# Strided sparse attention into an ELU feed-forward layer: batch 2 transposed by TensorE, some ELU clamps on ScalarE, batch 1 paced later

## The chip, the cores and the metric

The kernel runs on one core of one Trainium2 chip. The metric is the device time of the whole program in microseconds (us). A run also leaves a trace, whose span is about 1.7 us shorter than the time. A run counts as slow when it takes over 1.5% longer than the fastest of its kernel. A ratio is the mean time of one kernel's fast runs over the mean of the other's fast runs in the same rounds, so it is not quite the ratio of the medians that are quoted. The granted clock is the share of its full clock that TensorE was given in a stretch of a trace; where it is well below 1.00 the text calls it low or cold. SBUF is the core's working memory, PSUM the memory into which TensorE writes.

## The reference

Attention over 8 batches, 8 heads, 576 positions, head size 64, then a feed-forward layer on the 4608 tokens. Heads 0 to 3 see the last 32 positions ("local"), heads 4 to 7 every 32nd position ("strided").

```python
scores = np.matmul(q, k.transpose(0, 1, 3, 2)) / np.sqrt(64)
rel = pos[:, None] - pos[None, :]
mask_local = (rel >= 0) & (rel < 32)
mask_strided = (rel >= 0) & (pos[None, :] % 32 == pos[:, None] % 32)
attn = softmax(np.where(mask, scores, -1e9))       # heads 0-3 local, 4-7 strided
x = (attn @ v) as [4608 tokens, 512]
h = x @ w_in                                       # 512 -> 2048
g = np.where(h > 0, h, np.exp(np.minimum(h, 0)) - 1)
out = g @ w_out                                    # 2048 -> 512
```

## The kernel before

Queries and keys must stand with the head dimension on the partitions. For batches below `NPE` this is done by TensorE (a *T piece*: transposes into PSUM, then one VectorE copy each of q and k to SBUF). For the later batches DMA does it, from SBUF to SBUF. Attention of one batch is four head pairs; a pair is two *S pieces* (score matmuls, Exp, mask), each followed later by its *O part* (row sums, values, normalisation). A batch with T pieces runs T0 S0 T1 S0 S1 T2 S1 S2 T3 S2 S3 S3.

```python
def piece_T(P):
    for nm, dst in (("q", P.qT[:, 0:S]), ("k", P.kT[:, PRE:PRE + S])):
        ps = p_a.tile([128, S], BF16, tag="a", name="tp")
        # ... 8 (strided) or 16 (local) nc.tensor.transpose into ps ...
        nc.vector.tensor_copy(dst, ps)

def elu(hps, g):
    e = p_wk.tile([128, CHUNK], F32, tag="he", name="he")
    nc.scalar.activation(e, hps, ACT.Exp)
    e1 = p_wk.tile([128, CHUNK], BF16, tag="he1", name="he1")
    nc.vector.tensor_scalar(e1, e, scalar1=1.0, scalar2=1.0,
                            op0=ALU.min, op1=ALU.subtract)
    nc.vector.tensor_tensor(g, e1, hps, op=ALU.max)
```

The feed-forward layer of the first 512 tokens comes in one chunk: 16 groups of hidden-layer matmuls with ELU (`l1`), then 16 *slots*, each a quarter of an output tile (`l2`). Batch 1's twelve pieces are spread over the slots.

```python
for m in range(MC):
    l1(0, CHUNK, [m], g0[:, m, :], ...)
LATE = 5
for kk in range(CHUNK // 128):
    for part in range(4):
        l2(kk * 128, ..., part, spare=kk == 1)
        i = 4 * kk + part
        upto = first[1] + max(0, n * (i + 1 - LATE) // (16 - LATE))
        if done >= upto:
            flush()                       # the O parts still open
        while done < upto:
            run_piece(pieces[done], lag=1)
            done += 1
        if i == 2:
            fill_pad(2)                   # three small loads
            batch_in[2] = load_batch(2)
```

Everything after that is a stream of *steps*, from step 16 on. A step is one output quarter (`l2`; there are none in steps 16 to 23), then the attention pieces that are due, then one hidden-layer group (`l1`, 8 matmuls of 256 columns) with its ELU. Batch 2's attention has to be done in steps 23 to 29, batch 3's begins at step 32.

```python
dmaT_at[begin[1] + 1] = 2                 # DMA transposes of batch 2, step 17
for st in range(S0, NST):
    if todo:
        l2(*todo.pop(0))
    # ... lo, hi = step range of the next batch; upto as above ...
    while done < upto:
        run_piece(pieces[done], ...)
    l1(t0, TT, ..., p_a if st < S0 + SPT and j % 3 == 2 else None)
    # ... loads and DMA transposes of later batches ...
```

The softmax here doesn't subtract the row's maximum and nothing guards it: scores larger than these inputs give would overflow.

## Time and profile before

The median is 347.69 us of 3 runs (346.36 to 348.78); the traced run has a span of 346.4 us.

| stretch of the trace | what runs | what TensorE loses |
|---|---|---|
| 0 to 26 us | loads, attention of batch 0 | waits for loads; the change does not touch it |
| 26 to 42 us | hidden layer of the first chunk | little; VectorE is nearly full |
| 42 to 66 us | 16 slots with batch 1's attention | 1 us for ELU, then small gaps |
| 66 to 95 us | end of batch 1, steps 16 to 26, start of batch 2 | waits and a cold clock |
| 105 to 290 us | steady state | about 1% |
| 290 us to the end | the last output tiles | 4.8 us, much the same after the change |

The busy time by stretch of the kernel before. Columns: the stretch and its length, then the busy time and number of instructions of TensorE's matmuls (PE), weight loads, VectorE (DVE), ScalarE (ACT) and GpSimd; the granted TensorE clock; the DMA share; GB/s.

```profile
core 0: us, PE busy (x) PEld busy (x) DVE busy (x) ACT busy (x) POOL busy (x), PEclk, DMA share, GB/s
42.00:50.00 8.00, 6.95 (x45) 3.08 (x43) 5.30 (x11) 1.39 (x3) 2.95 (x4) 1.00 1.85 158
50.00:66.00 16.00, 14.49 (x220) 7.87 (x223) 9.39 (x19) 9.71 (x20) 11.40 (x16) 1.00 1.43 156
66.00:70.00 4.00, 1.67 (x26) 1.22 (x26) 2.55 (x6) 3.18 (x8) 3.65 (x5) 1.00 1.15 178
70.00:78.20 8.20, 7.68 (x53) 5.88 (x52) 5.61 (x11) 3.58 (x6) 2.75 (x4) 0.79 1.73 141
78.20:88.00 9.80, 5.05 (x47) 2.94 (x48) 4.15 (x9) 2.90 (x5) 1.38 (x2) 0.65 1.84 125
```

From 66 to 70 us TensorE is busy 1.67 of 4 us, and in the next stretch the clock is at 0.79; from 78.2 to 88 us it is busy 5.05 of 9.8 us, and the clock is at 0.65 in that stretch itself. A busy TensorE at clock 0.79 also does less: the 7.68 us of the fourth row hold only 53 recorded matmuls.

TensorE's waits, longest in total first, without the first loads at the start: instruction and line, what it waited for, us in total, times, longest.

```profile
...
PE sc L327 <- DMA ksT_114<-ks_89: 3.8, 1, 3.8
PE s_ps L370 <- DVE pm L343: 2.0, 4, 0.9
...
PE sc L327 <- ACT e L335: 1.4, 2, 0.7
PE sc L327 <- DMA klT_116<-kl_91: 1.4, 1, 1.4
...
PE ops L469 <- DVE g_511 L432: 1.0, 2, 0.8
```

TensorE in order of time near the longest wait: start, duration, line, names, count, and in brackets the idle time just before.

```profile
69.95 6.74 PE L441 MATMUL hps<-xT,w_in_sb 128*128 128x256 bf16 x45 [0.91 <-DVE xT L393]
77.20 1.03 PE L441 MATMUL hps<-xT,w_in_sb 128*128 128x256 bf16 x8 [0.52 <-DVE g L432]
82.03 0.42 PE L327 MATMUL sc<-qsT_113,ksT_114 64*128 64x72 bf16 x8 [3.79 <-DMA ksT_114<-ks_89]
...
83.55 1.89 PE L441 MATMUL hps<-xT,w_in_sb 128*128 128x256 bf16 x8
```

Batch 2's first score matmuls (`sc`) wait 3.79 us for a DMA transpose. Directly after it, 8 hidden-layer matmuls take 1.89 us; the same 8 took 1.03 us before the wait.

The chain of waits passes through another of batch 2's transposes, that of its local keys (`klT`), and the DMA view counts the packets:

```profile
62.44 8.72 DMA ks_93<-in_k_dram
72.43 6.02 DMA kl_95<-in_k_dram
78.44 15.59 DMA klT_116<-kl_91
```

Batch 2's queries and keys had landed by 65.4 us at the latest (the last is issued at 58.15 us and takes at most 7.2), before its transposes are issued from 67.15 us on. So TensorE waits for the transposes, which share the DMA engines with batch 3's loads, and not for batch 2's short loads.

```profile
DMA packets 104867, 36.16 MB, mean 104 GB/s; under 512 B 87296, under 2 KB 100224, under 8 KB 104832
```

### The profile page before, as it was taken

What the parts mean: (1) busy time and instruction counts of PE and PEld (TensorE: products, weight loads), DVE (VectorE), ACT (ScalarE), POOL (GpSimd) and SP (SyncE); (2) the same over time, 40 slices, a digit from 0 to 9 for tenths busy, and PEclk for the clock granted to TensorE, in tenths of its full rate; (3) what the DMA queues carried; (4) which work ended last, traced back from release to release, by engine and by line L of the source; (5) the groups of instructions that cost most, each with busy time, mean ns of one, the idle gap of its engine ahead of it and who ended that gap; (6) DMA issues with size and microseconds to landing.
All of it is one profiled execution on the core that took longest, in us unless ns stands there. A gap on an engine that the chain in (4) does not pass through costs nothing.

```text
span 346.4 us, 7372 instructions
## 1 busy us (share of the span) xinstructions
PE 315.0 (91%) x2835; PEld 196.6 (57%) x2880; DVE 233.7 (67%) x465; ACT 198.9 (57%) x377; POOL 80.0 (23%) x106
## 2 busy tenths in 40 slices
PE   1779989784899999999999999999999999999994
PEld 0554444462556666666566666666666666666661
DVE  2577955764687787676867778677767776666650
ACT  1575625742686676565655767676757675444431
POOL 7723246831073081102503034100000000000000
PEclk9999999986999999999999999999999999999999
DMA  6999999999999699911969329911921101111111
GB/s 87 153 206 207 175 169 160 149 148 134 109 144 172 113 106 134 195 42 35 132 116 150 79 45 174 158 38 32 153 55 38 38 22 42 46 32 30 40 53 62
DMA packets 104867, 36.16 MB, mean 104 GB/s; under 512 B 87296, under 2 KB 100224, under 8 KB 104832
## 3 DMA queue, kind: packets, MB, share of 16 engines
q0 software_dynamic: 68256, 18.58, 56.0%
q1 hardware_dynamic: 36576, 17.11, 28.6%
q8 instruction: 22, 0.36, 0.5%
q14 instruction: 13, 0.11, 0.1%
HBM read 37.09 MB, written 9.44 MB: 134 GB/s over the span
## 4 chain that ended last, share of the span: by engine, by line
PE 76%; DMA 11%; DVE 7%; issue 2%; POOL 2%; ACT 1%; DVEq 0%; POOLq 0%
PE hps L441 33%; PE ops L469 33%; DMA klT_116<-kl_91 5%; PE sc L327 3%; DVE g_511 L432 3%; DMA ks_93<-in_k_dram 3%; DMA kl_91<-in_k_dram 2%; PE s_ps L354 2%; DMA kl_95<-in_k_dram 2%; PE s_ps L370 2%; PE o_ps L375 1%; PE o_ps L363 1%; PE tp L292 1%; DVE kT_103 L299 0%; ACT osb L474 0%
## 5 line engine op out<-in xcount | busy, mean ns | idle before, releaser
L441 PE MATMUL hps<-xT,w_in_sb 128*128 128x256 bf16 (+1 forms) x1086 | 151.5, 285 | 2.0 <-DVE xT L393 0.9
L469 PE MATMUL ops<-w_out_sb,g 128*128 128x512 bf16 x473 | 124.8, 381 | 2.1 <-issue 0.2
L428 ACT ACTIVATE he<-hps 128x512 f32<-128x512 f32 x144 | 86.0, 597 | 63.9 <-PE hps L441 59.2
L441 PEld LDWEIGHTS <-w_in_sb 128*128 128x128 bf16 x1088 | 101.3, 99 | 36.2 <-issue 5.7
L469 PEld LDWEIGHTS <-g 128*128 128x128 bf16 x512 | 50.3, 98 | 35.1 <-issue 0.6
L335 ACT ACTIVATE e<-sc 72x576 bf16<-72x576 f32 (+1 forms) x60 | 38.6, 643 | 30.2 <-PE sc L327 30.1
L381 ACT ACTIVATE ln<-s_ps 128x288 f32<-128x288 f32 x64 | 26.2, 410 | 23.9 <-PE s_ps L354 14.0
L474 ACT COPY osb<-ops 128x512 f32<-128x512 f32 x36 | 21.1, 585 | 19.2 <-PE ops L469 18.9
L383 ACT ACTIVATE rc<-ln 128x288 f32<-128x288 f32 x64 | 28.3, 443 | 2.0
L87 POOL DMA_DIRECT2D vs<-in_v_dram x8 | 5.7, 707 | 69.8 <-PE o_ps L363 52.9
L388 DVE TENSOR_TENSOR xT<-o_ps,rc 128x288 bf16<-128x288 f32 x32 | 14.6, 458 | 9.3 <-ACT rc L383 8.5
L337 DVE TENSOR_TENSOR pm<-e,mask_s 72x576 bf16<-72x576 bf16 x32 | 14.6, 455 | 8.6 <-ACT e L335 7.7
L393 DVE TENSOR_TENSOR xT<-o_ps,rc 128x288 bf16<-128x288 f32 x32 | 14.6, 456 | 7.3 <-ACT rc L383 7.1
L128 POOL DMA_DIRECT2D vl<-in_v_dram x8 | 9.4, 1181 | 35.8 <-PE o_ps L375 31.9
L343 DVE TENSOR_TENSOR pm<-e,mask_l 128x576 bf16<-128x576 bf16 x32 | 14.7, 459 | 3.8 <-ACT e L335 3.2
L469 PE MATMUL ops<-w_out_sb,g_511 128*128 128x512 bf16 x60 | 15.3, 380 | 1.9 <-DVE g_511 L432 1.0
L370 PE MATMUL s_ps<-pm,ones 128*64 128x288 bf16 x64 | 10.5, 325 | 2.2 <-DVE pm L343 2.0
L375 PE MATMUL o_ps<-pm,vl 128*64 128x96 bf16 x192 | 11.1, 217 | 0.6 <-ACT ln L381 0.3
L370 PEld LDWEIGHTS <-ones 128*64 128x64 bf16 x64 | 3.8, 109 | 13.3 <-issue 10.5
L354 PEld LDWEIGHTS <-ones 72*64 72x64 bf16 x64 | 3.6, 110 | 13.1 <-issue 12.3
L354 PE MATMUL s_ps<-pm,ones 72*64 72x288 bf16 x64 | 10.7, 332 | 0.3 <-DVE pm L337 0.3
L375 PEld LDWEIGHTS <-vl 128*64 128x64 bf16 x192 | 9.3, 116 | 2.4 <-DVE vl L135 1.1
(379 smaller groups left out, 325.5 us busy)
## 6 DMA issues: line engine op xcount, KB each, us to landing
out_dram<-osb SPq DMA_DIRECT2D x32, 144.0 KB
vs<-in_v_dram POOLq DMA_DIRECT2D x8, 288.0 KB, 7.1
vl<-in_v_dram POOLq DMA_DIRECT2D x8, 288.0 KB, 7.8
w_in_sb<-in_moe_w_in_dram POOLq DMA_DIRECT2D x4, 512.0 KB, 13.7
w_out_sb<-in_moe_w_out_dram POOLq DMA_DIRECT2D x4, 512.0 KB, 20.2
qs_88<-in_q_dram POOLq DMA_DIRECT2D x4, 288.0 KB, 8.6
ks_89<-in_k_dram POOLq DMA_DIRECT2D x4, 288.0 KB, 9.7
qs_92<-in_q_dram POOLq DMA_DIRECT2D x4, 288.0 KB, 8.5
```

The costliest lines, as they stand in the source:

```text
L335: nc.scalar.activation(e[0:R], sc[0:R, :, 0:W], ACT.Exp, scale=scale)
L337: nc.vector.tensor_mul(pm[0:R].rearrange("p z (i n) -> p (z i) n", n=RS), e[0:R].rearrange("p z (i n) -> p (z i) n", n=RS), mask_s.unsquee ...
L343: nc.vector.tensor_mul(pm, e, mb.unsqueeze(1).to_broadcast([128, 2, W]))
L354: nc.tensor.matmul(s_ps[x * D:(x + 1) * D, :].rearrange("p (z n) -> p z n", z=2), lhsT=ones[0:RS, :], rhs=pv[:, x], start=True, stop=True, ...
L370: nc.tensor.matmul(s_ps[x * D:(x + 1) * D, :], lhsT=ones, rhs=pm[:, x], start=True, stop=True, skip_group_check=True)
L375: nc.tensor.matmul(o_ps[x * D:(x + 1) * D, i * LQ:(i + 1) * LQ], lhsT=batch_in[P.b]["vl"][:, (P.g0 + x) * LB + 3 * u + i, :], rhs=pm[:, x, ...
L381: nc.scalar.activation(ln, s_ps, ACT.Ln)
L383: nc.scalar.activation(rc, ln, ACT.Exp, scale=-1.0)
L428: nc.scalar.activation(e, hps, ACT.Exp)
L441: nc.tensor.matmul(hps[:, i], lhsT=w_in_sb[:, cc, m * 128:(m + 1) * 128], rhs=xT[:, cc, t0:t0 + nt], start=(c == 0), stop=(c == KC - 1))
L469: nc.tensor.matmul(ops, lhsT=g[:, m, :], rhs=w_out_sb[:, m, :], start=(m == 0), stop=(m == MC - 1))
L474: nc.scalar.copy(o_sb, ops)
```

## The change

The intent: take batch 2's transposes away from the DMA queue, relieve VectorE while ELU of the first tokens fills it, and leave two slots after batch 1's last piece to cover its latency. With e = exp(h), Relu(1 - e) on ScalarE is 1 - min(e, 1), the negative of what VectorE's clamp gives, so VectorE is left with one instruction per tile. Cut to its core:

```diff
-NPE = 2
+NPE = 3                        # batch 2: long loads, T pieces; its pad loads go
-    def elu(hps, g):
+    def elu(hps, g, on_act=False):
         nc.scalar.activation(e, hps, ACT.Exp)
+        if on_act:
+            nc.scalar.activation(e1, e, ACT.Relu, bias=1.0, scale=-1.0)
+            nc.vector.scalar_tensor_tensor(g, e1, -1.0, hps, op0=ALU.mult, op1=ALU.max)
+            return
-        l1(0, CHUNK, [m], g0[:, m, :], ...)
-    LATE = 5
+        l1(0, CHUNK, [m], g0[:, m, :], ..., on_act=m % 2 == 1)
+    LATE, END = 8, 14
-            upto = first[1] + max(0, n * (i + 1 - LATE) // (16 - LATE))
+            upto = first[1] + max(0, min(n, n * (i + 1 - LATE) // (END - LATE)))
             if i == 2:
-                fill_pad(2)
                 batch_in[2] = load_batch(2)
-    dmaT_at[begin[1] + 1] = 2
-            lo, hi = begin[b - 1] + (7 if b == 2 else 0), begin[b] - 2
+            lo, hi = begin[b - 1] + (4 if b == 2 else 0), begin[b] - 2
         l1(t0, TT, ...,
+           on_act=st < S0 + SPT and j % 2 == 1)       # every other step of 16 to 23
-            if load_at[st] == 3:
-                fill_pad(3)
+            if NPE <= load_at[st] < NPE + 2:
+                fill_pad(load_at[st])
```

Batch 2 now has twelve pieces instead of eight and begins at step 20.

More of the change, by code (lines that the diff above doesn't have):

```diff
@@ L432, in elu, with l1 @@
         nc.vector.tensor_tensor(g, e1, hps, op=ALU.max)
-    def l1(t0, nt, ms, g, pool=None):
+    def l1(t0, nt, ms, g, pool=None, on_act=False):
         hps = (pool or p_h).tile([128, len(ms), nt], F32,
@@ L444, in l1 @@
                     start=(c == 0), stop=(c == KC - 1))
-        elu(hps.rearrange("p a b -> p (a b)"), g)
+        elu(hps.rearrange("p a b -> p (a b)"), g, on_act)
     out_v = out.rearrange("(b p s) f -> b s p f", b=B, s=NS)
@@ L492 @@
     for m in range(MC):
-        l1(0, CHUNK, [m], g0[:, m, :], p_a if m % 5 > 1 else None)
-    LATE = 5
+        l1(0, CHUNK, [m], g0[:, m, :], p_a if m % 5 > 1 else None, on_act=m % 2 == 1)
+    LATE, END = 8, 14
     for kk in range(CHUNK // 128):
@@ L544 @@
            g[:, nm * j:nm * (j + 1), :].rearrange("p a b -> p (a b)"),
-           p_a if st < S0 + SPT and j % 3 == 2 else None)
+           p_a if st < S0 + SPT and j % 3 == 2 else None,
+           on_act=st < S0 + SPT and j % 2 == 1)
         if st in load_at:
-            if load_at[st] == 3:
-                fill_pad(3)
+            if NPE <= load_at[st] < NPE + 2:
+                fill_pad(load_at[st])
             batch_in[load_at[st]] = load_batch(load_at[st])
```

## The prediction

> **What bounds the kernel now.** TensorE is busy 315.0 of 346.4 us (busy totals). From 105.5 to 290 us it is busy 182.8 of 184.5 us (busy time by stretch), and neither the change's code nor its operands reach that part. What can be won lies before 105.5 us:
>
> - 42.1 to 105.5 us. Its warm work, from single durations in the timeline: 23 quarter output tiles at 0.865, 15 hidden-layer groups at 0.87, batch 1 attention about 8.0 us (3.1 of it transposes), batch 2 attention 4.9 us. Sum 45.9 of 63.4 us, so 17.5 us are lost.
> - 78.2 to 94.3 us: TensorE waits 3.79 us for a DMA transpose of batch 2's strided keys, 0.73 for an Exp, and 1.41 for that of the local keys; it is busy only 5.05 of 9.80 us to 88.0, at a granted clock of 0.65. The chain of waits names the same: 8.7 us load of keys, 6.0 us load of local keys, 15.6 us transpose.
> - 66 to 70 us: 0.69, 0.19, 0.87 and 0.91 us of waits on the latency chain of batch 1's last pieces; the clock then falls to 0.79, and 45 matmuls take 6.74 us where 4.9 would do.
> - 42 to 47 us: 1.0 us waiting for VectorE, which is 97% busy from 30 to 40 us with ELU (0.43 clamp + 0.69 max per tile against 0.865 us of matmuls).
>
> **What the change does.** It removes batch 2's four DMA transposes, issued from 67.1 to about 82.3 us, delays its three pad loads, and replaces eight loads of 256-byte runs by two of 1 to 2 KB runs: 87,296 of 104,867 packets are now under 512 B, a size that the Trainium skill, "DMA: Bandwidth & Descriptors", Specifications, puts below line rate. The pads occupy the queue from 36.2 to 43.4 us, so I expect batch 2 landed by about 62 us, before its first use near 70.
> It adds 96 TensorE transposes, 3.1 us (as batch 1's), and eight VectorE copies, 5.6 us (0.45 each, 1.43 for local keys), and packs batch 1's twelve pieces into six slots: about 3 us of small stalls, estimated from copy and Exp latencies.
> Relu on ScalarE: I estimate 0.6 to 0.7 us, as Exp has 0.60. It relieves VectorE by 0.43 on every other early tile and makes ScalarE nearly full; worth 1 to 1.3 us near 45 us.
>
> **Where it lands.** Hidden layer after batch 1 resumes near 68.4 instead of 69.95 us, at full clock (1.9 us more). Steps 20 to 23 are VectorE-bound, about 2 us per step. The first pieces of batch 2 no longer wait for DMA: about 8 us with the recovered clock, minus 3.1 us of transposes and 1.5 of new stalls. What ended at 105.5 us should end at 95 to 98.6. The remaining 241 us is unchanged.
>
> The clock part follows the Trainium skill, "TensorE: Matmul & The Clock Gate", Part 1: idle windows throttle the array. This trace agrees: 0.65 granted exactly where it waited.
>
> **Prediction:** 338.5 us, range 333.5 to 343.5 (8 in 10). Faster by over 2% (under 340.7): 0.68; within 2%: 0.31; slower: 0.01.
>
> **Signs.** Right: no wait of batch 2's score matmuls for a transpose; granted clock near 1.00 from 70 to 90 us; DMA transposes of batch 3 done before step 32; output matmuls no longer wait for the first ELU. Wrong: TensorE waiting for VectorE copies or score buffers between 50 and 66 us; batch 2's loads landing after 70 us; a clock drop still present there.
>
> **What would break it.** Stalls of the packed pieces could eat the gain in 50 to 66 us; VectorE could stay the limit in steps 16 to 24; batch 3's or batch 4's loads, delayed by the pads that moved, could put a new wait near 100 to 160 us.

## The result, and the profile after

The changed kernel takes 343.98 us (median of 4 runs, 343.36 to 344.51) against 347.85 us (4 runs) of the kernel before; ratio 0.9892, 95% interval 0.9853 to 0.9931. It is faster by about 1%, which is "within 2%", and the time lies just above the stated range. Run again in a later group on another chip it took 344.01 us, but the kernel before took 345.32 us there (11 runs), ratio 0.9959. The changed kernel repeats well; the kernel before moves by 2.5 us between groups. So the gain is 1.3 to 3.9 us, where 9.2 us were forecast.

The busy time by stretch after the change, columns as before:

```profile
42.00:50.00 8.00, 8.00 (x46) 3.74 (x45) 2.10 (x4) 2.55 (x5) 3.83 (x5) 1.00 1.70 183
50.00:66.00 16.00, 12.48 (x234) 7.71 (x233) 11.51 (x24) 10.13 (x21) 7.24 (x10) 1.00 1.40 184
66.00:70.00 4.00, 3.54 (x38) 2.59 (x36) 1.53 (x4) 2.86 (x7) 3.86 (x6) 1.00 1.93 132
70.00:78.20 8.20, 5.73 (x66) 4.61 (x65) 4.81 (x10) 4.10 (x7) 1.13 (x3) 0.79 1.37 171
78.20:88.00 9.80, 8.58 (x134) 6.16 (x134) 8.32 (x16) 7.28 (x16) 1.04 (x2) 1.00 0.90 110
```

The stretches 42 to 50, 66 to 70 and 78.2 to 88 us are fuller now; the packed pieces cost 2 us of TensorE's busy time from 50 to 66 us. But from 70 to 78.2 us TensorE is busy 5.73 of 8.2 us and the clock is again at 0.79. VectorE is idle for 3.4 of these 8.2 us too. The waits of the whole trace, without the first loads, and TensorE at that place:

```profile
...
PE sc L327 <- DVE kT_103 L299: 2.9, 2, 2.3
PE sc L327 <- DVE kT_101 L299: 2.1, 3, 0.9
PE sc L327 <- DVE kT_102 L299: 1.3, 2, 0.7
```

```profile
70.95 1.03 PE L445 MATMUL hps<-xT,w_in_sb 128*128 128x256 bf16 x8 [0.19 <-DVE g L436]
71.82 0.43 PE L284 MATMUL tp<-identity,qs_88 72*128 72x72 bf16 x8
72.08 0.43 PE L284 MATMUL tp<-identity,ks_89 72*128 72x72 bf16 x8
74.79 0.42 PE L327 MATMUL sc<-qT_106,kT_103 64*128 64x72 bf16 x8 [2.28 <-DVE kT_103 L299]
75.14 1.89 PE L445 MATMUL hps<-xT,w_in_sb 128*128 128x256 bf16 x8
```

The DMA wait of 3.79 us is gone, and in its place stand 2.28 us for a VectorE copy, with the same 1.89 us instead of 1.03 us behind it. VectorE over the same time shows why the copy is late:

```profile
71.81 0.42 DVE L434 TENSOR_SCALAR he_1145<-he 128x512 bf16<-128x512 f32 x1
72.34 0.69 DVE L436 TENSOR_TENSOR g<-he_1145,hps 128x512 bf16<-128x512 bf16 x1
73.31 0.69 DVE L432 SCALAR_TENSOR_TENSOR g<-he_1176,hps 128x512 bf16<-128x512 bf16 x1 [0.28 <-ACT he_1176 L431]
73.92 0.45 DVE L299 COPY qT_106<-tp 128x576 bf16<-128x576 bf16 x1
74.28 0.45 DVE L299 COPY kT_103<-tp 128x576 bf16<-128x576 bf16 x1
```

The transposes are in PSUM by about 72.5 us. TensorE has done four hidden-layer groups of steps 16 to 19 by then, and ELU has finished two of them. The copies start at 73.92 us, because the rest of ELU stands in front of them, its last instruction after a wait of 0.28 us for the new Relu on ScalarE. So 1.4 of the 2.28 us are ELU's arrears; the other 0.9 us are the two copies themselves, up to the first scores. The Trainium skill, "TensorE: Matmul & The Clock Gate", Part 1 (engine queue depths), says that ScalarE and VectorE are strict first-in, first-out; this trace agrees: both copies start only after the last of these instructions (73.92 us, after the one at 73.31).

The DMA view:

```profile
DMA packets 95427, 34.89 MB, mean 102 GB/s; under 512 B 76992, under 2 KB 90784, under 8 KB 95392
```

10,304 packets under 512 B are gone, and TensorE never waits for batch 2's loads. That packets under 512 B stay below line rate is what the Trainium skill's page "DMA: Bandwidth & Descriptors" (Specifications) says; no run here separates it from the pad loads and transposes that went at the same time.

Milestones on TensorE, one trace each (start in us of the first instruction):

| | before | after |
|---|---|---|
| batch 1's first transpose | 48.62 | 49.72 |
| hidden layer, step 16 | 68.54 (and again 69.95, after a wait) | 67.68 (no wait) |
| batch 2's first scores | 82.03 | 74.79 |
| output quarter of step 24 | 85.65 | 82.19 |
| batch 3's first scores | 108.15 | 104.10 |
| end of the span after that | 238.3 later | 238.1 later |

Batch 2's first scores come 7.2 us earlier, but step 24 only 3.5 (more pieces stand before it now, and the clock is low behind the wait), and the total gain is 4 us. After 104 us nothing changed.

### The profile page after: what moved, and what is told of

Its sections match the earlier page's. It is cut to its first block, busy times and chain, and to the rows that moved or that the text cites. A ratio compares the mean times of both kernels' runs of the same rounds, so it can differ in the third digit from the quotient of the medians.

```text
span 342.2 us, 7554 instructions
## 1 busy us (share of the span) xinstructions
PE 314.4 (92%) x2931; PEld 198.7 (58%) x2976; DVE 232.1 (68%) x461; ACT 205.3 (60%) x389; POOL 75.5 (22%) x100
## 4 chain that ended last, share of the span: by engine, by line
PE 63%; issue 17%; POOL 6%; DVE 5%; ACT 4%; DMA 3%; POOLq 0%; DVEq 0%
PE hps L445 29%; PE ops L473 26%; PE sc L327 3%; DMA kl_91<-in_k_dram 2%; PE s_ps L370 1%; DMA ql_90<-in_q_dram 1%; PE s_ps L354 1%; ACT e L335 1%; PE o_ps L375 1%; POOL ql_94 L102 1%; ACT he L428 1%; POOL kl_91 L118 1%; DVE kT_101 L299 1%; ACT ln L381 1%; POOL kl_95 L118 1%
## 5 line engine op out<-in xcount | busy, mean ns | idle before, releaser
L445 PE MATMUL hps<-xT,w_in_sb 128*128 128x256 bf16 (+1 forms) x1086 | 150.0, 283 | 0.8 <-issue 0.3
L473 PE MATMUL ops<-w_out_sb,g_511 128*128 128x512 bf16 x60 | 14.3, 380 | 0.6 <-issue 0.6
L363 PEld LDWEIGHTS <-vs 72*64 72x64 bf16 x256 | 10.0, 117 | 0.6
```

Source lines behind the costliest of these rows:

```text
L445: nc.tensor.matmul(hps[:, i], lhsT=w_in_sb[:, cc, m * 128:(m + 1) * 128], rhs=xT[:, cc, t0:t0 + nt], start=(c == 0), stop=(c == KC - 1))
L473: nc.tensor.matmul(ops, lhsT=g[:, m, :], rhs=w_out_sb[:, m, :], start=(m == 0), stop=(m == MC - 1))
```

## The experiments

Theory A: the forecast gain was lost at one place, where T0 and the scores that need it stand in one step; the copies between them queue behind ELU, TensorE waits 2.28 us, and the clock falls. Rival B: VectorE's work in steps 16 to 23 is simply too much (the prediction had said so, "about 2 us per step"), and a wait taken away there only moves. A second question is what each of the three parts does alone. All kernels gave correct results; each comparison is of 6 runs with 11 of the kernel before. One of the 11 beside e1 to e4 was slow (350.43 us): the ratios leave it out, and without it their median would be 345.80 us.

| run | median us | of before, same rounds | ratio (95%) |
|---|---|---|---|
| e1 clamps only | 344.87 | 346.04 | 0.9991 (0.9940 to 1.0042) |
| e2 pacing only | 345.84 | 346.04 | 1.0014 (0.9964 to 1.0064) |
| e3 TensorE transposes only | 346.82 | 346.04 | 1.0043 (0.9989 to 1.0097) |
| e4 changed, T0 early | 339.15 | 346.04 | 0.9825 (0.9781 to 0.9869) |
| e5 changed, gap filled | 341.83 | 345.48 | 0.9917 (0.9869 to 0.9965) |
| e6 e4, no clamps in steps 16 to 23 | 339.40 | 345.48 | 0.9845 (0.9801 to 0.9888) |
| e7 e4, old pacing | 340.55 | 345.48 | 0.9881 (0.9837 to 0.9926) |
| e8 all copies early | 341.81 | 345.48 | 0.9924 (0.9878 to 0.9970) |
| c1 changed kernel again | 344.01 | 345.32 | 0.9959 (0.9927 to 0.9991) |
| c2 e5 again | 342.15 | 345.32 | 0.9908 (0.9878 to 0.9939) |
| e9 transposes in their own buffers | 337.60 | 345.32 | 0.9773 (0.9742 to 0.9805) |
| e10 e4, no clamps at all | 341.24 | 345.32 | 0.9884 (0.9855 to 0.9913) |

The four lines from e1 on are one group, on one chip, and so are e5 to e8, and c1 to e10, each group on a chip of its own. One trace of a run also has its accident: the first output matmul starts at 40.49 to 42.35 us in the traces of kernels with the clamps and at 41.13 to 42.59 us without them. So the same points of two traces are compared from that start on.

### e1: only the clamps

```diff
 # the kernel before, with
+def elu(hps, g, on_act=False):   # Relu(1 - e) on ScalarE, max(-e1, h) on VectorE
+    l1(0, CHUNK, [m], ..., on_act=m % 2 == 1)
+       on_act=st < S0 + SPT and j % 2 == 1
```

> The kernel before with only the ScalarE clamps added. If the three parts simply add, this gives what was seen near 45 us: no wait of the first output matmuls for the first ELU (1.0 us) and about 1 us of total. In the stretch from 66 to 95 us the DMA transposes of batch 2 stay the limit, so nothing is gained there: 346.5 to 347.5 us. Rival: ELU on VectorE was a main limit of steps 16 to 23 too, then 344.5 or less.

No gain. Yet the clamps worked: the wait of the first output matmuls for ELU is gone, batch 1's first transpose starts at 45.67 us (48.62 before), and the hidden layer resumes at 67.02 us (69.95). Of these 3 us 1.6 lie before the first output matmul (40.49 against 42.09 us), where traces scatter that much; 1.35 us come after it. All of it ends at one line:

```profile
81.43 0.42 PE L327 MATMUL sc<-qsT,ksT 64*128 64x72 bf16 x8 [7.11 <-DMA ksT<-ks]
```

The DMA transpose arrives nearly when it did before (82.03 us), so TensorE, 3 us ahead, waits 7.11 instead of 3.79 us.

### e2: only the pacing

```diff
-    LATE = 5
+    LATE, END = 8, 14
-            upto = first[1] + max(0, n * (i + 1 - LATE) // (16 - LATE))
+            upto = first[1] + max(0, min(n, n * (i + 1 - LATE) // (END - LATE)))
```

> The kernel before with only batch 1's pieces packed into slots 8 to 13. The hidden layer resumes about 1 us earlier, at full clock, but the next wait, for batch 2's transposes near 79 us, takes it all back: within 0.5 us of the kernel before. Rival: pacing was a gain by itself, 1.5 us or more.

As expected, nothing. The hidden layer starts at 68.09 us without a wait, the clock stays at 1.00 up to 78.2 us, and then:

```profile
PE sc L327 <- DMA ksT<-ks: 5.1, 1, 5.1
```

### e3: only the transposes on TensorE

```diff
-NPE = 2
+NPE = 3
-                fill_pad(2)
-    dmaT_at[begin[1] + 1] = 2
-            lo, hi = begin[b - 1] + (7 if b == 2 else 0), begin[b] - 2
+            lo, hi = begin[b - 1] + (4 if b == 2 else 0), begin[b] - 2
 # and fill_pad for batches 3 and 4 instead of 2 and 3
```

> The kernel before with only batch 2 moved to long loads and TensorE transposes (with its start at step 20). The waits for DMA transposes (3.8 and 1.4 us) go, a wait for VectorE copies of the first piece appears, longer than the 2.3 us of the full change, since VectorE does all clamps: 344.5 to 346 us. Rival: this part carries all of the gain by itself, 344 us or less, and the other two parts nothing.

No gain either; the time is 0.8 us above what was expected. The DMA waits are gone, but the place of the 2.28 us wait has one of 2.40 us, and the clock is low before it too, since the old pacing leaves gaps of 0.69, 0.19, 0.88 and 0.48 us near 68 us (granted clock 0.50 from 70 to 74 us):

```profile
70.58 5.52 PE L441 MATMUL hps<-xT,w_in_sb 128*128 128x256 bf16 x29 [0.48 <-DVE xT L393]
...
79.03 0.42 PE L327 MATMUL sc<-qT,kT 64*128 64x72 bf16 x8 [2.40 <-DVE kT L299]
79.38 1.89 PE L441 MATMUL hps<-xT,w_in_sb 128*128 128x256 bf16 x8
```

The three parts alone give 0.9991, 1.0014 and 1.0043; their product is 1.0048, and together they give 0.9892 or 0.9959. They are not a sum: the first two win time ahead of a DMA that sets the pace, and the third takes that DMA away.

### e4: the changed kernel with one piece moved

```diff
             if i == 2:
                 batch_in[2] = load_batch(2)
+            if i == 15:
+                run_piece(pieces[first[2]])     # T0 of batch 2, before step 16
+                done += 1
```

> The changed kernel with one piece moved: the transposes of batch 2's first pair run in slot 15, before step 16, where VectorE is idle, instead of in step 20 just before the score matmuls that need them. Theory A: what ate the forecast gain is the 2.28 us wait of those score matmuls for copies that queue behind ELU on VectorE, and the cold clock after it (about 2 us more): the wait goes, granted clock stays at 0.95 or more from 72 to 78 us, and 339.5 to 341 us. Rival B: VectorE's total work in steps 16 to 23 is the limit, so the wait only moves to another instruction, and the time stays at 343 to 344 us.

339.15 us, 4.8 us less than the changed kernel, and a clear answer for theory A. The two medians come from different chips, but the changed kernel gave 343.98 and 344.01 us in two groups, and e10, which is e4 without the clamps, is 2.8 us ahead of it on one chip. The data were there: in the changed kernel's trace batch 2's first two loads, issued at 35.9 and 38.5 us, have landed by about 52 us. Slot 15 is a place where VectorE has little to do. VectorE's copy of k, then TensorE at step 20:

```profile
68.67 0.45 DVE L299 COPY kT<-tp 128x576 bf16<-128x576 bf16 x1
```

```profile
72.29 0.30 PE L327 MATMUL sc<-qT,kT 64*128 64x72 bf16 x8
72.53 1.05 PE L445 MATMUL hps<-xT,w_in_sb 128*128 128x256 bf16 x8
```

No wait, and the next 8 matmuls take 1.05 us. From 70 to 78.2 us TensorE is busy 7.80 of 8.2 us at clock 1.00, and VectorE 7.13 instead of 4.81 us: it had room. From these scores to the output quarter of step 24 (78.08 us) four steps, now without T0, take 5.8 us, or 1.45 us each.

### e5 and c2: the same wait, with a busy array

```diff
             run_piece(pieces[done], ...)
+            if done == first[2]:                # between T0 and its scores
+                fill = p_o.tile([128, d_model], F32, tag="o", name="fill")
+                for _ in range(10):
+                    nc.tensor.matmul(fill, lhsT=w_out_sb[:, 0, 0:128],
+                                     rhs=w_in_sb[:, 0, 0:512], start=True, stop=True)
             done += 1
```

> The changed kernel with ten 512-column matmuls of no use (about 2.2 us at full clock) between the transposes and the score matmuls of batch 2's first pair, where TensorE now waits 2.28 us. The wait stays as long but the array is busy in it. If the cold clock after the wait is half of the cost, the granted clock stays near 1.00 from 70 to 80 us and the time falls by 1.5 to 2.2 us, to about 342 us, although work was added. Rival: the clock costs nothing and only the wait does: the time stays or grows by up to 0.3 us.

> e5 again, on the same chip as the changed kernel. If the cold clock after the 2.28 us wait costs time by itself, this is 1.5 to 2.2 us faster than the changed kernel of this group although it does ten matmuls more. Rival: the difference seen in e5 (341.83 against 343.98 us) was one of chips, then within 0.5 us of it.

> The changed kernel itself, so that it stands on one chip beside the other runs of this group. If times compare across groups, 343.5 to 344.5 us. If the chip matters by more than 1 us, the comparisons of e4 to e8 with it have to be made from this run.

The first look, 341.83 against 343.98 us, compared two chips. Beside each other on one chip, the changed kernel takes 344.01 and the filled one 342.15 us: ten matmuls of no use save 1.86 us. The stretch from 70 to 78.2 us and the first scores of batch 2, of the changed kernel (c1) and of the filled one (c2):

```profile
70.00:78.20 8.20, 5.73 (x63) 4.44 (x61) 4.89 (x11) 3.50 (x6) 1.13 (x3) 0.73 1.49 179
```

```profile
74.16 0.42 PE L327 MATMUL sc<-qT,kT 64*128 64x72 bf16 x8 [2.28 <-DVE kT L299]
74.51 1.89 PE L445 MATMUL hps<-xT,w_in_sb 128*128 128x256 bf16 x8
```

```profile
70.00:78.20 8.20, 7.74 (x101) 5.48 (x100) 6.00 (x12) 4.80 (x10) 1.74 (x3) 1.00 1.48 135
```

```profile
73.63 0.30 PE L327 MATMUL sc<-qT,kT 64*128 64x72 bf16 x8
73.87 1.05 PE L445 MATMUL hps<-xT,w_in_sb 128*128 128x256 bf16 x8
```

From T0's first transpose to the scores both take 2.97 us, so only the clock differs. Of the 4.8 us that e4 wins, then, 1.9 us are the clock after the wait and 2.3 us the wait itself. The traces agree: from the first output matmul to batch 3's first scores the changed kernel takes 62.15 us and e4 57.99, which is 4.2 us. The last 0.6 us of the medians, from two chips, is not accounted for.

### e6, e7 and e10: e4 with one part taken back

```diff
 # e6: l1 in steps 16 to 23
-           on_act=st < S0 + SPT and j % 2 == 1)
+           )
 # e7
-    LATE, END = 8, 14
+    LATE, END = 5, 16
 # e10: as e6, and for the first chunk
-    l1(0, CHUNK, [m], ..., on_act=m % 2 == 1)
+    l1(0, CHUNK, [m], ...)
```

> e4 (first transpose early, 339.15 us) with the clamps of steps 16 to 23 back on VectorE; those of the first chunk stay on ScalarE. If VectorE's load limits these steps once the wait is gone, TensorE waits for VectorE again there and the time is 1 to 2 us longer, 340.2 to 341.2. Rival: the load was never the limit, within 0.3 us of e4.

> e4 with the old pacing of batch 1 (slots 5 to 15). The last pieces are not covered any more: 0.7, 0.2, 0.9 and 0.5 us of waits before the hidden layer, but the 3.3 us of small stalls of the packed pieces go, and the first transposes of batch 2 fill part of the gap. I expect the same within 1 us: 338.5 to 340 us. Rival: the late pacing is what the full change needed, then 341 us or more.

> e4 without any clamp on ScalarE. Of the first chunk's clamps only the wait of the first output matmuls for ELU is left to win (1.0 us before), since eight plain output slots stand between ELU and batch 1's first piece: 340.0 to 340.5 us. Rival: as in e1, where they brought the pieces 3 us forward, then 341.5 us or more.

e6: 339.40 us, the same as e4. Putting VectorE's load of steps 16 to 23 back (four clamps of 0.43 us, more than the two copies of 0.45 us that e4 took away) costs nothing, so rival B falls a second time, and the late half of the clamps is worth nothing. e7: 340.55 us, 1.4 us more than e4, a bit above what was expected: the late pacing is worth something once nothing downstream absorbs it, mostly by keeping the clock up (0.79 from 66 to 70 us with the old pacing, 1.00 in e4). Against e6, on the same chip, it is 1.15 us. e10: 341.24 us, 2.1 us more than e4, between the two expectations. One part of it is plain, the wait for ELU that came back:

```profile
46.43 4.71 PE L473 MATMUL ops<-w_out_sb,g 128*128 128x512 bf16 x21 [0.67 <-DVE g L436]
```

With 0.19 us more just before it, that is 0.9 us. In the traces batch 1's first transpose starts 1.1 us later than in e4 (50.97 against 49.87), and batch 3's first scores 1.25 us later; the rest of the 2.1 us is not explained. e4 and e10 ran on different chips; their ratios differ by the same 0.6%, but the intervals overlap.

### e8: every copy early, and a miss

```diff
+    # batches 1 and 2: T0 T1 S0 S0 T2 S1 S1 T3 S2 S2 S3 S3
+    SLOT = {6: 1, 7: 1, 8: 1, 9: 1, 10: 2, 11: 2, 12: 1, 13: 2, 14: 1}
-            upto = first[1] + max(0, min(n, ...))
+            upto = done + SLOT.get(i, 0)
     flush()
# batch 2's pacing then counts these two as done
+    for _ in range(2):                          # T0 and T1 of batch 2
+        run_piece(pieces[done])
+        done += 1
```

> A version meant to be the best: every pair's transposes run at least a slot before the score matmuls that read them, for batches 1 and 2 (batch 1 in slots 6 to 14, two transposes of batch 2 after slot 15). If the 0.65 us stalls of score matmuls for copies in 50 to 66 us (three of them) and the one for a buffer go: 2 to 3 us less than e4, 336.3 to 337.5 us, and no wait over 0.4 us for a copy. Rival: the buffers of the transposes, shared with the attention outputs, make new waits of the same size: 338.5 us or more.

341.81 us, worse than e4 by 2.7 us (than e6, on the same chip, by 2.4); the rival was right. No wait for a copy is left, but the T pieces share three PSUM buffers with the O parts, and the new order makes them wait for those:

```profile
77.34 0.45 PE L292 MATMUL tp<-identity,ql 72*64 72x72 bf16 x16 [1.27 <-ACT ln L381]
```

The clock fell after this gap too: the next 8 hidden-layer matmuls take 1.89 us.

### e9: the version that beats both

```diff
 # e4, with
-            ps = p_a.tile([128, S], BF16, tag="a", name="tp")
+            ps = (p_h if P.b == 1 else p_a).tile(
+                [128, S], BF16, tag="h" if P.b == 1 else "a", name="tp")
-    LATE, END = 8, 14
+    SLOT = {6: 1, 7: 2, 8: 1, 9: 2, 10: 1, 11: 2, 12: 1, 13: 2}
-            upto = first[1] + max(0, min(n, ...))
+            upto = done + SLOT.get(i, 0)
```

> e4, with batch 1's transposes one slot ahead of their use (slots 6 to 13) and in the accumulators of the hidden layer, idle in that stretch, so that they share no buffer with the attention outputs. e8's new waits were for those shared buffers. The 0.65 us stalls for copies and the one for a buffer go, the one of the last pair (0.33) stays: 2 to 3 us less than e4's 339.15, 336.3 to 337.3 us. Rival: the stalls come from ScalarE's and VectorE's chain of the packed pieces, and return at other instructions, 338.5 us or more.

337.60 us (336.33 to 338.56), between the two expectations; ratio 0.9773 to the kernel before, and 6.4 us less than the changed kernel on the same chip. The piece order is the old one, only cut so that T0 stands one slot ahead of its scores, and batch 1's transposes use the hidden layer's accumulators, which are idle between 42 and 64 us. The hidden layer starts at 64.79 us (68.35 in e4), and batch 3's first scores at 96.53 us (100.09). One copy wait of 0.55 us and one of 0.59 us, which the profile puts down to ScalarE's Ln, remain. But not all of these 3.56 us are won by the edit: the first output matmul, ahead of everything that was changed, starts at 40.49 us here and at 42.10 us in e4.

```profile
40.49 6.21 PE L474 MATMUL ops<-w_out_sb,g 128*128 128x512 bf16 x28
...
42.10 7.93 PE L473 MATMUL ops<-w_out_sb,g 128*128 128x512 bf16 x36
```

From there to the hidden layer e9 (first line) takes 24.30 us and e4 (second line) 26.25: the edit wins 1.95 us, near the 1.55 us between the medians. The traced run of e9 is the fastest of its six, that of e4 the slowest.

## Why the prediction was wrong, point by point

- **The range failed because of one term, "1.5 of new stalls" for batch 2.** The step was "about 8 us with the recovered clock, minus 3.1 us of transposes and 1.5 of new stalls". The waits on batch 2's pieces from 71 to 88 us are 2.28, 0.29, 0.45 and 0.37 us, 3.4 us together, and the cold clock after the first adds 1.9 us (c1 and c2): 5.3 us in place of 1.5. With this the four steps 20 to 23 take 10.4 us (71.82 to 82.19). The sum closes: 6.9 us of gain by its upper end (below), less these 3.8 us, and 0.7 more because the hidden layer resumed at 67.68 and not at 68.4 us, makes 3.8; measured were 4.05.
- **"Granted clock near 1.00 from 70 to 90 us" was wrong.** It is 0.79 from 70 to 78.2 us. The prediction recovered the clock that the DMA wait had lost and did not ask whether the wait put in its place would lose it again.
- **"Steps 20 to 23 are VectorE-bound, about 2 us per step" was wrong in kind.** VectorE was busy 4.81 of 8.2 us there. The engine was not too slow; a dependent pair stood too close together behind its queue. e4 moved one piece and these steps took 1.45 us each; e6 put load back on VectorE without effect. The prediction knew that the copies go through VectorE and counted their 5.6 us, but not their place in line.
- **Also the centre promised too much.** "What ended at 105.5 us should end at 95 to 98.6" came from a careful sum at its upper end (98.6, a gain of 6.9 us, that is 340.8 us) while its lower end had no term behind it; the centre was set between. Batch 3's first scores give the measured gain, 4.05 us.
- **Clamps, "1 to 1.3 us near 45 us": right there.** From the first output matmul to batch 1's first transpose the kernel before takes 6.53 us and e1 5.18, 1.35 less (whether the clamps also bring that first matmul forward is not shown); taken from e4, the clamps cost 1.1 us at that place (e10). That the medians of e10 and e4 differ by 2.1 us is in part unexplained. ScalarE's Relu takes 0.63 us, inside the estimate of 0.6 to 0.7; ScalarE is busy 13.2 of 16 us from 26 to 42 us (before 9.1), as said.
- **Right:** no score matmul of batch 2 waits for a transpose by DMA any more; output matmuls no longer wait for the first ELU; batch 2's loads land in time; about 3 us of stalls from the packed pieces (3.5 us idle from 50 to 66 us); the hidden layer resumes earlier, and even without the wait that was expected (67.68 us against 68.4); no new wait near 100 to 160 us; the last 238 us unchanged. And so was the warning about "TensorE waiting for VectorE copies": between 50 and 66 us, where it was put, there are three such waits of about 0.65 us, but the expensive one came at 72.5 us.

## What to carry to other kernels

When a slow transfer is replaced by on-chip work, look at where the first consumer stands: a copy needed at once joins the end of an in-order engine's queue, behind the arrears that stand there (here 1.4 us of ELU). Place such a piece one phase earlier, where that engine is idle; here one moved piece was worth 4.8 us by the medians and 4.2 us by the traces, the whole change 1.3 to 3.9. And do not add the gains of parts that stand in front of the same wait: alone the three parts gave nothing, because the next wait took it back, and a long wait on TensorE has to be counted with the cold clock behind it: in these traces each wait of 2.28 us or more (the first loads aside) was followed by 8 matmuls in 1.89 us, while after one of 1.41 us, at 94 us in the kernel before, they took 1.05.

## What the Trainium skill lacked or had wrong

- "TensorE: Matmul & The Clock Gate", Part 1 and the table at the page's end, warns of idle gaps of more than about 3 us. Here shorter ones were enough: one of 2.28 us, one of 1.27 us together with one of 0.67 us three us earlier (e8), and four of 0.69, 0.19, 0.88 and 0.48 us within 4 us (e3; clock 0.50 from 70 to 74 us). The kernel before, e1 and e7 have nearly the same four gaps and soon after them a clock of 0.50, 0.50 and 0.56 over 2 us. How long several short gaps must be together, the page does not say. If transposes do not count as work for the clock, as Part 4 of the page suggests, the first of these gaps is 2.97 us long (71.82 to 74.79 us); no run here tests that. The page's half clock agrees: 8 matmuls took 1.89 us instead of 1.03 us. Filling the 2.28 us with useless matmuls saved 1.86 us (c1 and c2).
- "ScalarE: Activation LUTs", Rules for kernel authors, sends Relu to VectorE. Per instruction that is right (clamp 0.43 us on VectorE, Relu 0.63 us on ScalarE), but with VectorE at its limit and ScalarE not, moving every other clamp of the first chunk was worth 1.1 us where it acts, by the traces, and 2.1 us by medians from two chips (e10 against e4).
- "VectorE: DVE Perf Modes" gives copy rates for dense patterns and says that the doubled mode needs steps of one element. The copy of 128x576 bf16 from PSUM took 0.45 us in order and 1.43 us when the local keys were written with a step of four: 3.2 times as long. The page has no figure for such steps, and no page has one for such a copy out of PSUM.
- No page tells that the time of a kernel whose TensorE waits in its middle scatters more. The six runs of e3 lie 4.2 us apart, those of e4 1.3 us. In e3 the time follows the mean granted clock of the run: 348.81 us at 0.977, 347.7 at 0.984 and 0.985, 345.95 at 0.990, 344.58 and 345.62 at 0.995; e4's runs are all at 0.997 to 1.000. The clock is not the only source: e9's runs lie 2.2 us apart at 0.997 to 1.000.
